# Turning the queries of two tiles with one DMA transpose in an attention and ReGLU kernel

## The chip, the core and the metric

The kernel runs on one core of a Trainium2 chip. The metric is the device time of one launch in microseconds (us). Before the change the median of three runs is 1029.53 us (1028.31 to 1029.58).

## The reference

Attention with keys and values that are pooled in space, followed by a feed-forward block with a ReLU gate. Everything has 128 channels:

```python
B, C, Hh, Ww = (4, 128, 384, 32)          # q: (4, 12288, 128), kv: (4, 384, 32, 128)
kv_pool = kv.reshape(B, H // r, r, W // r, r, C).mean(axis=(2, 4))   # r = 4
kv_flat = kv_pool.reshape(B, -1, C) @ w_sr                           # 768 rows for each image
k = v = kv_flat
s = scale * (q @ k.transpose(0, 2, 1))
a = np.exp(s - s.max(-1, keepdims=True))
a /= a.sum(-1, keepdims=True) + 1e-09
x = (a @ v).reshape(B * S, D)                                        # 49152 x 128
out = np.maximum(x @ w_gate, 0.0) * (x @ w_val) @ w_out              # d_ff = 1536
```

## The kernel before

The 49152 query rows are cut into 96 tiles of 512 rows (T), 24 for each image. Four tiles make a group (GRP), so there are 24 groups. `k` numbers tiles, `g = k // 4` groups, and `ph = k % 4` is the phase of a tile in its group.

**What happens to a tile.** Its queries are loaded from HBM by GpSimd's DMA, which casts them to float16 (`q_load`, L133, a whole group in four transfers, into the tile `q16`, two buffers). Rows lie on the partitions then, and the scores need the channels there, so the queries are turned by a DMA transpose on SyncE's queue (`q_turn`, L149, issued in L155) into `qT` (three buffers, a group each). Blocks of 128 queries are multiplied with the 768 keys (`score_block`, L359), ScalarE takes the exponential and its row sums (`exp_block`, L364), and the weights `a` are turned by two DMA transposes for each tile, on the same queue of SyncE (`a_turn`, L391), into `aT` (four buffers). TensorE multiplies them with the values (`values`, L401), VectorE stores the result as `xT` (L409), and then come twelve value and gate projections (L455, L468), their combination on ScalarE and VectorE (L462, L476), the product with w_out (L496), a transpose on VectorE (L504), the scaling on GpSimd (L509), and the store, by DMAs from SyncE and GpSimd (L741). The division by the row sums is put off to that scaling.

**What sets the order.** The order is written out by hand: lists of words say what each engine's queue gets next. The first four tiles are mixed into the opening, which also pools and projects the keys of the first image. Then a loop (L719) runs over steps `k` from 4 to 98, and each step deals with several tiles at different stages: the scores of tile `k`, the values of tile `k - 2`, the projections of tile `k - 3`, the output of tile `k - 4`. The lists are FIRST, STEADY and DRAIN. Beside this work, keys and values of the next image are loaded and pooled (`image_step`, L706) in the first half of each image's steps. Every queue runs its instructions in the order in which they are written here, and an instruction that waits holds up the ones behind it.

**The query turns.** They are issued at the head of a step, ahead of everything else that the step puts on SyncE's queue: the turned weights, half of the stores, the loads of keys and values. In the steps of group `g`, phase 1 turns tile 0 of group `g + 1`, phase 2 tile 1, phase 3 tile 2; tile 3 of a group is turned in phase 0 of its own steps. Groups 0 and 1 are partly turned in the opening, the rest of group 1 by one instruction at L722. In phase 1, after the turn, GpSimd's queue gets the loads of group `g + 2`, into the buffer of `q16` that the last turn of group `g` has read.

The lines which decide on that are these:

```python
        if ph == 0 and g > 1:
            q_turn(g, GRP - 1)
        elif ph > 0:
            q_turn(g + 1, ph - 1)
        if ph == 1:
            q_load(g + 2)
```

Of the kernel before, what the change touches and what calls it, by code (L numbers as in the profile page):

```python
# [16 lines left out]
def kernel(  # L17
# [34 lines left out]
    NS = T // 128  # L52
    NST = N // T
    NT = B * NST
    GRP = 4
# [77 lines left out]
    def q_load(g):  # L133
        if not 0 <= g < NG:
            return
        b, n0 = divmod(g * GRP * T, N)
        q16 = work.tile([128, GRP * NS, C], FP16, tag="q16", bufs=2)
        rows = q[b, n0 : n0 + GRP * T, :]
        if g == NG - 1:
            nc.gpsimd.dma_start(q16, rows.rearrange("(p s) c -> p s c", p=128))  # L140
        else:
            rows = rows.rearrange("(i t j s) c -> j t i s c", i=GRP, t=32, s=NS)
            for j in range(4):
                nc.gpsimd.dma_start(  # L144
                    q16[32 * j : 32 * (j + 1)].rearrange("t (i s) c -> t i s c", i=GRP), rows[j]
                )
        q16s[g] = q16

    def q_turn(g, i):  # L149
        if not 0 <= g < NG:  # L150
            return
        if g not in qTs:
            qTs[g] = work.tile([128, GRP * NS, 128], FP16, tag="qT", bufs=3, name="qT")
        at = slice(i * NS, (i + 1) * NS)
        nc.sync.dma_start_transpose(  # L155
            qTs[g][:, at], q16s[g][:, at].rearrange("p s c -> p (s c)")
        )
        if i == GRP - 1:
            del q16s[g]

    def q_load_pair(i):
# [218 lines left out]
    def spread_scales(k, j):  # L380
        if j == 0:
            scales[k // 2] = work.tile([128, 2, NS * 4], FP32, tag="scale", bufs=3, name="scale")
        to = scales[k // 2].rearrange("t e (s j) -> t e s j", j=4)
        for b in range(4):
            nc.gpsimd.tensor_copy(  # L385
                to[32 * b : 32 * (b + 1), :, :, j], squares[k // 2][32 * j : 32 * (j + 1)]
            )
# [99 lines left out]
    def out_proj(k, fb):  # L487
        if k >= NT - 3:
            if fb == 0:
                o_banks[k] = bank([128, NS, 128])  # L490
            for s in range(NS):
                out_add(k, fb, s, o_banks[k][:, s, :], fb == 0 and s == 0)
            return
        if fb == 0:
            o_banks[k] = bank([128, T])
        nc.tensor.matmul(  # L496
            o_banks[k], wo16[:, fb, :], hTs[k][:, fb, :], start=fb == 0, stop=fb == NFB - 1
        )

    def out_turn(k):  # L500


        o_t = work.tile([128, T], FP32, tag="o_t", bufs=2)
        nc.vector.transpose(o_t, freed(o_banks.pop(k)))  # L504
        o_sb = work.tile([128, 4, NS, 32], FP32, tag="o_sb", bufs=3)
        o_by = o_t.rearrange("t (s j c) -> t s j c", s=NS, j=4)
        to = o_sb.rearrange("t j s c -> t s j c")
        scale = scale_of(k).rearrange("t (s j o) -> t s j o", s=NS, o=1)
        nc.gpsimd.tensor_tensor(to, o_by, scale.to_broadcast([128, NS, 4, 32]), op=ALU.mult)  # L509
        del hTs[k]  # L510
        g = k // GRP
        rows = out[g * GRP * T : (g + 1) * GRP * T, :]
        moves = []
        for b in range(4):
            o_b = o_sb[32 * b : 32 * (b + 1)]
            if g == 0:
                to = rows.rearrange(
                    "(e j t i s) (b c) -> e b i j t s c", e=2, j=4, t=32, s=NS, c=32
                )
                moves += [(to[k // 2, b, k % 2, j], o_b[:, j]) for j in range(4)]  # L520
            elif g == NG - 1:
                to = rows.rearrange("(j t i s) (b c) -> b i j t s c", j=4, t=32, s=NS, c=32)
                moves += [(to[b, k % GRP, j], o_b[:, j]) for j in range(4)]
            else:
                to = rows.rearrange("(i t r) (b c) -> b i t r c", t=32, r=16, c=32)
                moves.append((to[b, k % GRP], o_b.rearrange("t j s c -> t (j s) c")))
        return moves

    def out_scale(k, engine, own, o_ps=None):
        if k not in o_sbs:  # L530
            o_sbs[k] = work.tile([128, NS, 128], FP32, tag="o_sb", bufs=3, name="o_sb")
        o_sb, o_ps = o_sbs[k][:, own], o_ps if o_ps is not None else freed(o_banks[k])
        scale = squares[k // 2][:, k % 2, own]
        if engine is nc.scalar:
            for s in range(o_sb.shape[1]):
                nc.scalar.mul(o_sb[:, s], o_ps[:, s], scale[:, s : s + 1])
        else:
            nc.vector.tensor_tensor(
                o_sb, o_ps, scale.rearrange("t (s o) -> t s o", o=1).to_broadcast(list(o_sb.shape)),
                op=ALU.mult,  # L540
            )
# [164 lines left out]
    def image_step(b, at, step):  # L706
        for pair in range(NJC // 2):
            since = at - 4 * pair
            if since in (0, 1) and step in (2, 8):
                kv_load(b, pair, [2 * since + step // 8])  # L710
            elif since in (3, 4) and step == 3:
                pool_pixels(nc.gpsimd, b, pair, since - 3)
            elif since == 6 and moves and step > 4:
                nc.sync.dma_start(*moves.pop())
            elif since in (9, 11) and step == 1:
                turn_values_dma(b, 2 * pair + since // 11)

    last = NT + LAG - 1
    for k in range(LEAD, last + 1):  # L719
        g, ph = divmod(k, GRP)  # L720
        if k == GRP:
            nc.sync.dma_start_transpose(  # L722
                qTs[1][:, 2 * NS :], q16s.pop(1)[:, 2 * NS :].rearrange("p s c -> p (s c)")
            )
        if ph == 0 and g > 1:
            q_turn(g, GRP - 1)
        elif ph > 0:
            q_turn(g + 1, ph - 1)
        if ph == 1:
            q_load(g + 2)  # L730
        b = k // NST + 1
        at = k % NST - 4
        kO, kF, kV = k - LAG - 1, k - LAG, k - 2
        words = FIRST if kV < LEAD else STEADY if k < NT else DRAIN if k < last else LAST
        for word in words:
            head, n = word.rstrip("0123456789"), int(word.lstrip("abcdefghijklmnopqrstuvwxyzADPT") or 0)
            if head == "o":
                out_proj(kO, n)
                for queue in (nc.gpsimd, nc.sync):
                    if out_moves and n >= 2:  # L740
                        queue.dma_start(*out_moves.pop())  # L741
                if spread:
                    spread_scales(*spread.pop(0))
                if b < B:
                    image_step(b, at, n)
            elif head == "oT":
                if kO < NT - 3:
                    out_moves = out_turn(kO)
                elif k < last:
                    out_scale(kO, nc.vector, slice(0, NS))  # L750
                    out_store(kO, slice(0, NS))
            elif head in ("v", "y", "g", "h"):
                if kF < NT:
                    {"v": value_proj, "y": keep_value, "g": gate_proj, "h": gated}[head](kF, n)
            elif head in ("s", "e"):
                if k < NT:
                    {"s": score_block, "e": exp_block}[head](k, n)
                    if head == "e" and n % 2:
                        a_turn(k, n - 1, n + 1)
            elif head == "r":  # L760
                if LEAD < k <= NT and k % 2 == 0:
                    invert(k - 2)
                    spread += [(k - 2, j) for j in range(4)]
            elif head in ("tb", "P", "pk"):
                pair, since = divmod(at - 6 if head == "tb" else at - 8, 4)
                if b < B and 0 <= pair < NJC // 2 and since == 0:
                    if head == "tb":
                        moves.extend(turn_blocks(b, pair))
                    elif head == "P":
                        project(b, pair)  # L770
                    else:
                        keep_projected(b, pair)
            elif LEAD <= kV < NT:
                if head == "x":
                    values(kV, n)
                else:
                    keep_values(kV)
# [33 lines left out]
```

The softmax here doesn't subtract the row's maximum and nothing guards it: scores larger than these inputs give would overflow.

## Time and profile before

| | before |
|---|---|
| median of 3 runs | 1029.53 us |
| span of the profiled run | 1027.5 us |
| PE, ACT, DVE, POOL busy | 99%, 90%, 84%, 51% |
| DMA bytes | 153.51 MB |
| query turns in the loop (L155) | 88 |
| issue of one on SyncE's queue: shortest, median, longest | 1.19, 1.75, 5.27 us |
| issue to landing of one: shortest, median, longest | 2.5, 4.1, 10.7 us |
| weight turns (L391) | 184, median issue 1.47 us, median 4.8 us to landing |

PE is TensorE, ACT ScalarE, DVE VectorE, POOL GpSimd, and SP SyncE; a q behind a name (SPq) means the engine's queue of instructions, which also issues DMAs. The busy time of PE counts matmuls which overlap, so the question is not how busy it is but where it waits. A DMA has two times: how long its instruction holds the queue, and how long it is until the data has landed. In a group of the profile, "out<-in" are the program's names for what an instruction writes and reads, and "A <- B" in the list of waits means that A stood idle until B was done.

### The profile page before, as it was taken

What the parts mean: (1) busy time and instruction counts of PE and PEld (TensorE: products, weight loads), DVE (VectorE), ACT (ScalarE), POOL (GpSimd) and SP (SyncE); (2) the same over time, 40 slices, a digit from 0 to 9 for tenths busy, and PEclk for the clock granted to TensorE, in tenths of its full rate; (3) what the DMA queues carried; (4) which work ended last, traced back from release to release, by engine and by line L of the source; (5) the groups of instructions that cost most, each with busy time, mean ns of one, the idle gap of its engine ahead of it and who ended that gap; (6) DMA issues with size and microseconds to landing.
All of it is one profiled execution on the core that took longest, in us unless ns stands there. A gap on an engine that the chain in (4) does not pass through costs nothing.

```text
span 1027.5 us, 17571 instructions
## 1 busy us (share of the span) xinstructions
PE 1020.5 (99%) x5048; PEld 489.5 (48%) x5048; DVE 862.5 (84%) x1432; ACT 920.1 (90%) x1931; POOL 525.1 (51%) x1308
## 2 busy tenths in 40 slices
PE   9999999999999999999999999999999999999998
PEld 5444444444444444444444444444444444444445
DVE  2888888888888888888888888888888888888887
ACT  5999998899999999999999999989999999999986
POOL 3588766434446585535434856654334443343342
PEclk9999999999999999999999999999999999999999
DMA  9999998999998998979879899898696897867641
GB/s 327 155 160 162 182 186 141 143 150 148 140 171 170 192 169 167 159 125 141 129 123 209 152 178 190 157 144 140 120 141 108 144 129 123 130 122 110 113 83 43
DMA packets 476721, 153.51 MB, mean 149 GB/s; under 512 B 452944, under 2 KB 466768, under 8 KB 476624
## 3 DMA queue, kind: packets, MB, share of 16 engines
q1 hardware_dynamic: 454592, 126.08, 68.6%
q0 software_dynamic: 21600, 25.19, 17.2%
q10 hardware_dynamic: 432, 1.11, 0.3%
q8 instruction: 40, 0.66, 0.3%
q14 instruction: 57, 0.47, 0.2%
HBM read 53.94 MB, written 26.35 MB: 78 GB/s over the span
## 4 chain that ended last, share of the span: by engine, by line
PE 97%; DMA 2%; ACT 1%; issue 0%; SPq 0%; DVE 0%; DVEq 0%
PE bank_ps L455 24%; PE bank_ps L468 24%; PE bank_ps L496 23%; PE bank_ps L401 12%; PE wide_ps L359 11%; DMA aT<-a 1%; DMA q<-in_q_dram 1%; PE bank_ps L482 1%; PE bank_ps L344 1%; PE bank_ps L418 0%; PE bank_ps L270 0%; PE wide_ps L302 0%; ACT a L364 0%; PE bank_ps L284 0%; ACT val L462 0%
## 5 line engine op out<-in xcount | busy, mean ns | idle before, releaser
L476 DVE SCALAR_TENSOR_TENSOR hT<-bank_ps,val 128x512 f16<-128x512 f32 x1152 | 728.2, 680 | 105.6 <-PE bank_ps L468 84.0
L462 ACT CAST val<-bank_ps 128x512 f16<-128x512 f32 x1149 | 628.3, 595 | 45.6 <-PE bank_ps L455 25.0
L455 PE MATMUL bank_ps<-xT,wv 128*128 128x512 f16 x1152 | 420.5, 379 | 0.1
L468 PE MATMUL bank_ps<-xT,wg 128*128 128x512 f16 x1152 | 375.9, 379 | 0.0
L496 PE MATMUL bank_ps<-hT,wo 128*128 128x512 f16 x1116 | 348.4, 379 | 0.0
L364 ACT ACTIVATE a<-wide_ps 128x768 f16<-128x768 f32 x368 | 302.0, 821 | 44.9 <-PE wide_ps L359 44.9
L359 PE MATMUL wide_ps<-kv,qT 128*128 128x512 f16 x736 | 179.7, 326 | 0.1
L401 PE MATMUL bank_ps<-aT,kv 128*128 128x512 f16 x552 | 178.8, 379 | 0.7 <-DMA aT<-a 0.6
L496 PEld LDWEIGHTS <-wo 128*128 128x128 f16 x1116 | 109.2, 98 | 131.9 <-issue 0.7
L468 PEld LDWEIGHTS <-wg 128*128 128x128 f16 x1152 | 112.7, 98 | 122.4 <-issue 0.5
L509 POOL TENSOR_TENSOR o_sb<-o_t,scale 128x512 f32<-128x512 f32 x89 | 93.2, 1047 | 137.9 <-issue 120.2
L455 PEld LDWEIGHTS <-wv 128*128 128x128 f16 x1152 | 112.7, 98 | 106.0 <-issue 1.7
L385 POOL COPY scale<-square 32x8 f32<-32x8 f32 x736 | 141.2, 192 | 28.6
L741 POOL DMA_DIRECT2D out_dram<-o_sb x216 | 134.8, 627 | 19.0 <-POOL o_sb L509 13.0
L378 POOL TENSOR_TENSOR square<-inverse 128x8 f32<-128x8 f32 x46 | 9.3, 202 | 249.0 <-DVE inverse L376 249.0
L359 PEld LDWEIGHTS <-qT 128*128 128x128 f16 x736 | 72.0, 98 | 87.1 <-issue 0.4
L409 DVE CAST xT<-bank_ps 128x512 f16<-128x512 f32 x92 | 63.6, 691 | 32.4 <-PE bank_ps L401 32.4
L401 PEld LDWEIGHTS <-kv 128*128 128x128 f16 x552 | 54.0, 98 | 66.5 <-issue 1.6
L364 ACT ACTIVATION_READ_ACCUMULATOR a<-wide_ps 128x1 f32 x368 | 75.9, 206 | 0.0
L504 DVE STREAM_TRANSPOSE o_t<-bank_ps 128x512 f32<-128x512 f32 x93 | 65.4, 704 | 0.0
L144 POOL DMA_DIRECT2D q<-in_q_dram x84 | 46.7, 573 | 15.6 <-DMA qT<-q 14.7
L237 POOL TENSOR_TENSOR s<-kv_in 128x512 f32<-128x512 f32 x36 | 45.2, 1285 | 1.5 <-DMA kv_in<-in_kv_dram 0.8
(78 smaller groups left out, 205.8 us busy)
## 6 DMA issues: line engine op xcount, KB each, us to landing
kv_in<-in_kv_dram SPq DMA_DIRECT2D x42, 512.0 KB, 4.7
out_dram<-o_sb SPq DMA_DIRECT2D x177, 64.0 KB, 2.6
out_dram<-o_sb POOLq DMA_DIRECT2D x176, 64.0 KB, 4.3
q<-in_q_dram POOLq DMA_DIRECT2D x84, 128.0 KB, 6.6
aT<-a SPq DMA_TRANSPOSE x184, 4.8
kv_line<-in_kv_dram SPq DMA_DIRECT2D x4, 512.0 KB, 9.9
qT<-q SPq DMA_TRANSPOSE x91, 4.1
placed<-blocks SPq DMA_DIRECT2D x9, 128.0 KB, 1.9
```

What stands on the lines that cost most here:

```text
L359: nc.tensor.matmul(s_ps[:, j0 * 128 : j1 * 128], qT, kv16[:, b, j0:j1, 0:C], start=True, stop=True)
L364: nc.scalar.activation(a16s[k][:, s, :], s_banks.pop(s)[:, 0:J], AF.Exp, scale=qk_scale, accum_out=a_sums[k // 2][:, k % 2, s : s + 1],)
L385: nc.gpsimd.tensor_copy(to[32 * b : 32 * (b + 1), :, :, j], squares[k // 2][32 * j : 32 * (j + 1)])
L401: nc.tensor.matmul(x_banks[k], kv16[:, k // NST, jc, C : 2 * C], aT[:, jc], start=first, stop=x_left[k] == 0,)
L455: nc.tensor.matmul(proj_banks["v", k, fb], wv16[:, fb * 128 : (fb + 1) * 128], xTs[k], start=True, stop=True,)
L462: (nc.vector.tensor_copy if k < LEAD - 1 and fb == 5 else nc.scalar.copy)(vals[k, fb], freed(proj_banks.pop(("v", k, fb))))
L468: nc.tensor.matmul(proj_banks["g", k, fb], wg16[:, fb * 128 : (fb + 1) * 128], xTs[k], start=True, stop=True,)
L476: nc.vector.scalar_tensor_tensor(hTs[k][:, fb, :], freed(proj_banks.pop(("g", k, fb))), 0.0, vals.pop((k, fb)), op0=ALU.max, op1=ALU.mult,)
L496: nc.tensor.matmul(o_banks[k], wo16[:, fb, :], hTs[k][:, fb, :], start=fb == 0, stop=fb == NFB - 1)
L504: nc.vector.transpose(o_t, freed(o_banks.pop(k)))
L509: nc.gpsimd.tensor_tensor(to, o_by, scale.to_broadcast([128, NS, 4, 32]), op=ALU.mult)
L741: queue.dma_start(*out_moves.pop())
```

## The change

A query turn takes two neighbouring tiles at a time. It is issued in phase 1 (tiles 0 and 1 of the next group) and in phase 3 (tiles 2 and 3), and none in phases 0 and 2. It is meant to halve the number of these instructions on SyncE's queue, and it frees the buffer of a group's loaded queries in the step before the group's own steps begin, not in the first of them.

```diff
-    def q_turn(g, i):
+    def q_turn_two(g, i):
         if not 0 <= g < NG:
             return
         if g not in qTs:
             qTs[g] = work.tile([128, GRP * NS, 128], FP16, tag="qT", bufs=3, name="qT")
-        at = slice(i * NS, (i + 1) * NS)
+        at = slice(i * NS, (i + 2) * NS)
         nc.sync.dma_start_transpose(
             qTs[g][:, at], q16s[g][:, at].rearrange("p s c -> p (s c)")
         )
-        if i == GRP - 1:
+        if i == GRP - 2:
             del q16s[g]
...
-        if ph == 0 and g > 1:
-            q_turn(g, GRP - 1)
-        elif ph > 0:
-            q_turn(g + 1, ph - 1)
+        if ph % 2:
+            q_turn_two(g + 1, ph - 1)
         if ph == 1:
             q_load(g + 2)
```

## The prediction

> **What bounds the kernel now.** I read the page's busy shares first, then the busy time by stretches, the list of waits, and last the SyncE queue's timeline where that list pointed. From the page:
>
> ```profile
> PE 1020.5 (99%) x5048; PEld 489.5 (48%) x5048; DVE 862.5 (84%) x1432; ACT 920.1 (90%) x1931; POOL 525.1 (51%) x1308
> ...
> q1 hardware_dynamic: 454592, 126.08, 68.6%
> ...
> PE 97%; DMA 2%; ACT 1%; issue 0%; SPq 0%; DVE 0%; DVEq 0%
> ```
>
> TensorE is busy 99% of the span, and the chain that ended last runs over it for 97%. A busy TensorE need not be one at its peak, so I looked for the time that it really loses. The busy time by stretches (columns: stretch, its length, then busy time and count of PE, PEld, DVE, ACT, POOL, clock, DMA share, GB/s):
>
> ```profile
> 38.00:62.00 24.00, 23.89 (x116) 11.20 (x115) 21.10 (x35) 23.22 (x51) 12.74 (x22) 1.00 1.08 185
> 62.00:230.00 168.00, 167.35 (x807) 79.27 (x806) 143.37 (x239) 152.21 (x321) 108.78 (x247) 1.00 0.95 159
> 230.00:640.00 410.00, 409.98 (x1978) 194.09 (x1977) 350.57 (x580) 374.35 (x788) 226.00 (x550) 1.00 0.94 160
> 640.00:1000.00 360.00, 360.00 (x1737) 170.13 (x1735) 308.52 (x510) 328.75 (x691) 155.06 (x436) 1.00 0.77 127
> ```
>
> Between 38 and 1000 us TensorE is idle for 0.11 + 0.65 + 0.02 + 0.00 = 0.78 us. Shorter waits could hide under the overlapping ends of matmuls, so I also looked at the starts in the timeline: 512-column matmuls start 0.216 us apart, the first value product (L401) of one tile follows that of the tile before by 10.37 us almost everywhere (10.80 where a key projection is added), and the exceptions add up to 0.27 us near 55.6, 0.17 at 156, 0.81 at 187.7 and 0.25 near 427. So between opening and end at most 1.5 us are lost, and 0.98 of it (156 and 187.7) on turned weights, aT. Everything else is the matmuls' own pace, which the change doesn't touch.
>
> The waits name the one place where a transpose held TensorE, and the one where a query turn held anybody:
>
> ```profile
> POOL q L144 <- DMA qT<-q: 14.7, 3, 7.2
> ...
> PE bank_ps L401 <- DMA aT<-a: 0.6, 1, 0.6
> ```
>
> The SyncE queue around that stall (start, length, count of merged instructions):
>
> ```profile
> 167.53 3.32 SPq L391 DMA_TRANSPOSE aT<-a  x2
> 170.90 1.59 SPq L155 DMA_TRANSPOSE qT<-q  x1
> 172.58 1.65 SPq L741 DMA_DIRECT2D out_dram<-o_sb  x2
> 174.32 3.88 SPq L391 DMA_TRANSPOSE aT<-a  x2
> 178.37 4.49 SPq L155 DMA_TRANSPOSE qT<-q  x1
> ```
>
> Its instructions follow each other without a hole. The weights of tile 16 were ready when ScalarE ended its last exponential at 168.5, but their second turn was issued at 175.90 and landed 12.63 us later, at 188.5; the product that reads it started 0.65 us late. So from about 80 to 220 us the queue runs some 5 to 16 us behind its inputs. Taking landing times from the trace, the spare time between the landing of a tile's aT and its first reader is 0.1 us for tiles 13 and 16, 0.9 to 1.3 for 8, 10, 12 and 14, 2.6 and 2.7 for 15 and 9; the median over all tiles is 11.7, and from tile 22 on it is never under 7.
>
> **What the Trainium skill says.** "DMA: Bandwidth & Descriptors", section "Rules for kernel authors", advises to coalesce many small transfers into a large one. A one-tile turn moves 128x512 float16, 131 KB, a joint one 262 KB, so only the fixed part is to be saved. "Perfetto Trace Analysis", section "DMA Instruction — HWDGE (DVE, Sync)", says that such an instruction's profiled time is the generation of its descriptors and not the moving, and that its wait is done by the sequencer before it. The trace agrees: the shortest query turn takes 1.19 us on the queue and 2.5 us to landing. "DMA: Bandwidth & Descriptors", section "Issuing engines are not separate DMA queues", says that GpSimd's and SyncE's transfers share the same engines; here the aT turn at 175.90 landed after 12.63 us, against a median of 4.8, just when GpSimd's four query loads had been issued from 175.64.
>
> **The change part by part.**
>
> *Fewer instructions.* Groups 2 to 23 have 4 turns each, the row's 88; now 2 each, 44. Bytes stay. Lone issue time hardly depends on size: at best 1192 ns for the 4 blocks of a query turn, 1273 ns for the 12 of an aT turn, so 10 ns for a block and 1.23 us for 8 blocks. That is the lower bound of a joint turn. The upper one: the queue is held back by the engines. q1 moved 126.08 MB in 68.6% of 1027.5 us, 179 GB/s, so 131 KB more cost 0.73 us; added to the median single turn of 1.745 us this gives 2.48 us. Two single ones take 3.49, so a pair saves 1.0 to 2.2 us of queue time, 44 pairs 44 to 99 us; I take 1.5, 66 us. Off the path nearly everywhere: TensorE waits for this queue once. It counts only in the backlog from 62 to 230 us, some 16 steps and 8 pairs: 8 to 18 us saved there, as much as the backlog itself. So I expect the spare times there to grow by some us, and the 0.65 us stall (0.81 by the starts) to shrink or vanish.
>
> *Where the turns stand.* Before: tile 0 of the next group at phase 1, 1 at phase 2, 2 at phase 3, 3 at phase 0 of its own group. Now 0 and 1 at phase 1, 2 and 3 at phase 3. No tile is turned later than before; each is turned three or four steps (31 or 41 us) ahead of its scores, against a longest landing of 10.7 us. No reader gets a new wait: 0. The buffers: qT's third one was last read a group earlier (0), and the query load that a joint turn needs was issued four steps before (landing at most 10.8 us): 0.
>
> *What waits behind.* In phases 1 and 3 the joint turn stands ahead of that step's two aT turns; these come up to 0.73 us later by it. In phases 0 and 2 they come 1.2 to 1.75 us earlier. On balance a gain: of the six tiles with under 1.3 us to spare, five are in phases 0 and 2 and only tile 13 in phase 1, with a whole turn (1.56 us at 126.57) gone from the step before it.
>
> *The query load.* q_load(g+2) at phase 1 takes the buffer that the last turn of group g frees. That turn now stands two steps earlier, so GpSimd's three waits, 3.33, 7.25 and 4.09 us, 14.7 together, end. GpSimd is 51% busy and nobody is named as waiting for it on the path, so this is worth 0 directly. But these three loads go out earlier, and each is a burst that stretches aT turns. This part I cannot size from the trace of before; both ends follow below.
>
> *Sum.* −0.65 us times a good chance that it goes, about −0.5, and nothing else on the path: 1029.53 − 0.5 = 1029.0 us.
>
> **The rivals.**
>
> *A: the load's burst hits a tight tile.* The load of group 6 moves from 175.64 to 168.4, into the landing of tile 15's turns (issued 167.53 and 169.10, read at 177.50). If the second takes 12.63 us as tile 16's did, it lands at 181.7: 4.2 us of stall instead of 0.65, so 1029.53 + 3.6 = 1033.1 us, slower than before by 0.3%. For it: the collision is the very one that caused the stall before. Against it: the queue by then issues these turns 1 to 3 us sooner, before the load, and the other two moved loads (3.33 and 4.09 us earlier) newly meet tiles (11 and 19) with over 6 us to spare. A milder form, 1 to 2 us on one or two tiles, gives 1030 to 1031.5.
>
> *B: all waits in the steady part vanish.* Then 1.5 us go, 1028.0 us, still within 0.2%. Only the 0.98 us on aT has anything to do with the change, so this needs luck in the waits at 55.6 and 427 too.
>
> *C: faster by over 0.2%.* This needs 2.06 us, more than TensorE loses between 38 and 1000 us. Opening and end have no part that the change moves: the first changed turn is issued at about 49 us, and the last turn only moves from 952 us to some 10 us before. Only scatter of the runs (1028.31 to 1029.58) could show it.
>
> *D: single waits shift but the sum stays.* 1029.5 us; it cannot be told from my forecast.
>
> **How the numbers follow.** Forecast with D: 0.72, at 1029.0. B: 0.10. A in its mild form: 0.07; A in full, or a stall like it elsewhere, over 1031.6: 0.08. C: 0.03. The range from 1027.8 (B less a little of the scatter) to 1031.2 (most of mild A) leaves out C, full A and a little at the edges, some 0.14. The bounds on the joint turn's issue (1.23 to 2.48 us) don't widen it, as both save queue time. Faster by over 0.2% 0.04, within 0.2% 0.86, slower 0.10.
>
> **What would show it.** Right: 44 turns of 8 blocks with a median issue between 1.23 and 2.48 us; no wait of GpSimd's query load for a query turn; the three loads issued near 126, 168 and 211 us; TensorE still busy 99%, tiles still 10.37 us apart; no or less wait for aT; DMA bytes as before. Wrong: waits of L401 for aT of several us between 60 and 230 us (A), a joint turn holding the queue over 3.5 us in the median, so that nothing is saved, or scores (L359) waiting for qT.

## The result, and the profile after

The change makes the kernel faster: 1026.62 us in the median of 12 runs (1026.31 to 1027.44), against 1029.55 us (1028.20 to 1031.37) for the kernel before, a ratio of 0.9975 with a 95% interval of 0.9967 to 0.9983. That is 2.9 us less. The forecast was 1029.0 us with a range of 1027.8 to 1031.2, and "faster by over 0.2%" had a chance of 0.04. Beside the median, the spread shrank, from 3.2 to 1.1 us.

From the page of the kernel after:

```profile
PE 1019.4 (100%) x5048; PEld 489.5 (48%) x5048; DVE 861.8 (84%) x1432; ACT 919.9 (90%) x1931; POOL 524.8 (51%) x1308
...
q1 hardware_dynamic: 453184, 126.08, 67.7%
...
PE 98%; DMA 1%; ACT 1%; SPq 0%; issue 0%
```

The bytes of q1 are the same, and so is the work of every engine. The busy time by stretches of the kernel after (same columns as in the prediction):

```profile
38.00:62.00 24.00, 23.89 (x117) 11.24 (x115) 21.09 (x36) 23.16 (x51) 12.22 (x22) 1.00 1.02 195
62.00:230.00 168.00, 168.00 (x812) 79.82 (x810) 144.13 (x241) 153.00 (x322) 109.07 (x248) 1.00 0.94 164
230.00:640.00 410.00, 409.98 (x1978) 194.05 (x1977) 350.50 (x579) 374.40 (x788) 225.29 (x549) 1.00 0.91 159
640.00:1000.00 360.00, 360.00 (x1736) 170.12 (x1735) 308.30 (x510) 328.23 (x690) 155.94 (x439) 1.00 0.74 125
```

In the second row TensorE's 167.35 us have become 168.00 of 168.00. In the list of waits, GpSimd's query load no longer waits for a turn, and the value product no longer waits for aT. In a second profile of this kernel (below) it does not either. The query turns themselves, all instructions of line 155 (shortest, median and longest time on the queue, in ns, then issue to landing):

```profile
L155 SPq DMA_TRANSPOSE qT<-q x44: 1314/1784/5349, 48.2 to 939.8; - x44
...
DMA to landing us min/median/max: 3.4/5.5/9.1
```

A joint turn holds the queue for 1.78 us in the median, where a single one took 1.75. Summed over the trace, query turns take 88.6 us of SyncE's queue instead of 174.9. Part of that is taken up again: between 62 and 230 us, all instructions that issue DMAs together held the queue for 152.8 us of the 168 before, and for 141.0 and 143.9 us in the two profiles after, as the weight turns then took longer. The queue at the place that the prediction showed:

```profile
162.18 3.32 SPq L391 DMA_TRANSPOSE aT<-a  x2
165.59 1.52 SPq L739 DMA_DIRECT2D out_dram<-o_sb  x2
167.20 4.59 SPq L391 DMA_TRANSPOSE aT<-a  x2
171.97 5.35 SPq L155 DMA_TRANSPOSE qT<-q  x1
```

Tile 16's two weight turns now start at 167.20 and 168.89; they started at 174.32 and 175.90. The second one landed 8.5 us before its reader, where it had held the reader up.

**Where the 3.0 us between the two profiled spans went.** The first value products of the tiles in the loop, L401, are good marks, as TensorE's order is the same in both kernels.

| stretch | before | after | difference |
|---|---|---|---|
| start to the first L401 | 62.46 us | 61.68 us | -0.78 |
| first L401 to that of the last tile | 940.67 us | 939.70 us | -0.97 |
| that one to the end | 24.38 us | 23.16 us | -1.22 |

The middle row is what the prediction hoped to gain from, and its size is what was allowed there. Two thirds, 2.00 us, lie in the start and the end. Both profiled executions took about their kernel's median (1029.29 and 1026.33 us of launch time), so the table can stand for a typical execution. There were two questions for the experiments: is 0.97 us the usual loss of the kernel before, and do the start and the end have anything to do with the change?

### The profile page after: what moved, and what is told of

Its sections match the earlier page's. It is cut to its first block, busy times and chain, and to the rows that moved or that the text cites. A ratio compares the mean times of both kernels' runs of the same rounds, so it can differ in the third digit from the quotient of the medians.

```text
span 1024.5 us, 17514 instructions
## 1 busy us (share of the span) xinstructions
PE 1019.4 (100%) x5048; PEld 489.5 (48%) x5048; DVE 861.8 (84%) x1432; ACT 919.9 (90%) x1931; POOL 524.8 (51%) x1308
## 3 DMA queue, kind: packets, MB, share of 16 engines
q0 software_dynamic: 21600, 25.19, 15.9%
## 4 chain that ended last, share of the span: by engine, by line
PE 98%; DMA 1%; ACT 1%; SPq 0%; issue 0%
PE bank_ps L455 24%; PE bank_ps L468 24%; PE bank_ps L496 23%; PE bank_ps L401 12%; PE wide_ps L359 12%; DMA q<-in_q_dram 1%; PE bank_ps L482 1%; PE bank_ps L344 1%; PE bank_ps L418 1%; PE bank_ps L270 0%; PE wide_ps L302 0%; PE bank_ps L284 0%; ACT a L364 0%; ACT val L462 0%; PE bank_ps L432 0%
## 5 line engine op out<-in xcount | busy, mean ns | idle before, releaser
L401 PE MATMUL bank_ps<-aT,kv 128*128 128x512 f16 x552 | 178.9, 379 | 0.0
L401 PEld LDWEIGHTS <-kv 128*128 128x128 f16 x552 | 54.0, 98 | 65.1
```

What stands on the lines that cost most here:

```text
L401: nc.tensor.matmul(x_banks[k], kv16[:, k // NST, jc, C : 2 * C], aT[:, jc], start=first, stop=x_left[k] == 0,)
```

## The experiments

### The kernel before once more

No edit.

> The kernel before, unchanged, for a second profile. The gain of 2.9 us splits in the two profiles into 0.78 us before the first value product of the loop (L401), 0.97 us between the first and the last tile's, and 1.25 us after it. If the first and the last part are properties of the program, this profile has them as before: first L401 near 62.5 us, some 24.4 us from the last tile's first L401 to the end, and a ratio of 1.000. If they are scatter of single executions, they move here by some tenths of a us or more, and only the 0.97 us need an explanation from the program.

Measured: 1029.07 us, ratio 0.9999 (0.9992 to 1.0005). The start takes 62.46 us and the end 24.23 us, much as before. But the middle took 942.09 us, 2.4 us more than 939.70. The waits of TensorE in this profile (total, times, longest) and the busy time from 62 to 230 us:

```profile
PE bank_ps L401 <- DMA aT<-a: 1.9, 3, 1.2
```

```profile
62.00:230.00 168.00, 166.09 (x800) 78.49 (x799) 142.25 (x237) 151.03 (x318) 110.17 (x249) 1.00 0.93 159
```

The same program, and TensorE idles three times instead of once, before tiles 8, 12 and 13; in the first profile it idled before tile 16, and tile 13 came 0.17 us late. What follows: the loss is drawn anew in each execution. It does not follow that the first profile had an unusually small one. The second profiled execution took 1030.57 us, 1.5 us more than the median of its own kernel, and the first 1029.29 us. If the 1.5 us lie in the middle, where the two profiles differ, a typical execution loses some 0.9 us there (2.39 less 1.5, an estimate).

### Joint turns early, joint turns late

```diff
-        if ph == 0 and g > 1:
+        if ph == 0 and g > 1 and not (g < 6):            # late: not (g >= 6)
             q_turn(g, GRP - 1)
-        elif ph > 0:
+        elif ph > 0 and not (g + 1 < 6):                 # late: not (g + 1 >= 6)
             q_turn(g + 1, ph - 1)
+        elif ph % 2:
+            q_turn(g + 1, ph - 1, 2)                     # two tiles
```

(`q_turn` takes the number of tiles as its third argument here.)

> Joint turns for groups 2 to 5 alone (8 instructions fewer), single ones from group 6 on. Theory 1 (queue time of SyncE in the backlog up to 230 us): the aT stalls go, 0.98 us less between first and last L401, 1028.6 us. Theory 2 (the end of the program: semaphores of the last DMAs and instruction fetches, which shift with the count of DMAs; 8 fewer leave the eight semaphores in the same turn): the end stays at 24.4 us here, and the gain is no more than 1 us. If the whole gain of 2.9 us came from the early stretch, it would be 1026.6 us.

> Joint turns from group 6 on alone (36 instructions fewer, which moves the last DMAs by four of the eight semaphores as the change does). Theory 1: the stall before tile 16 and the slip before tile 13 stay, no gain between first and last L401. Theory 2: the end gets 0.3 to 1.2 us shorter, 1028.4 to 1029.3 us. If both hold, this gain and that of the early pairs add up to about 2.2 of the 2.9 us.

Measured: early pairs 1027.64 us, ratio 0.9983 (0.9974 to 0.9992); late pairs 1028.78 us, ratio 0.9993 (0.9984 to 1.0001). From 62 to 230 us, first of the early pairs, then of the late ones:

```profile
62.00:230.00 168.00, 168.00 (x812) 79.90 (x811) 144.07 (x240) 153.00 (x322) 109.23 (x249) 1.00 0.91 165
```

```profile
62.00:230.00 168.00, 165.11 (x795) 78.03 (x794) 141.26 (x234) 150.17 (x316) 108.17 (x246) 1.00 0.94 156
```

Eight instructions fewer in groups 2 to 5 remove every stall in this profile: the middle takes 939.70 us, to the hundredth what it takes in the kernel after. (One of the 18 executions took 1034.72 us; nothing was recorded of what held it up.) The gain, 1.6 us in the medians, is not that of the middle alone. The profiled execution took 1027.69 us, 1.60 us less than the one before; of this the middle has 0.97 us, the start 0.46 and the end 0.72 us. Against them stands launch time outside the profiled span: in all 18 executions it was 2.2 to 2.3 us, and 1.7 to 2.0 us in all executions of every other kernel. Where this half microsecond goes, no run shows. With late pairs the middle keeps its stalls (943.07 us), and the start and the end, 61.83 and 23.23 us, are about those of the kernel after. So the stalls belong to the early groups; the start and the end are shorter in both. 1.6 and 0.5 us add up to 2.1 of the 2.9 us, but such gains need not add up.

### The same places, but one tile each

```diff
-        if ph == 0 and g > 1:
-            q_turn(g, GRP - 1)
-        elif ph > 0:
-            q_turn(g + 1, ph - 1)
+        if ph % 2:
+            q_turn(g + 1, ph - 1)
+            q_turn(g + 1, ph)
```

> The turns where the change has them (phases 1 and 3), but one instruction for each tile, 88 as before. Theory 1 (fewer instructions on the queue): the backlog stays and so do stalls of tiles 13 and 16, perhaps larger as two turns stand in a row in phases 1 and 3: 1029.5 us or slower. Rival (the earlier release of the loaded queries' buffer, so that GpSimd's waits of 14.7 us for a turn end): the stalls go here as with the change, 0.98 us less between first and last L401, 1028.6 us. Count of DMAs as before, so the end stays at 24.4 us.

Measured: 1030.32 us, ratio 1.0013 (1.0001 to 1.0025), slower than before if anything. TensorE waits for aT before tiles 13 and 15; the middle takes 941.78 us.

```profile
PE bank_ps L401 <- DMA aT<-a: 1.8, 2, 1.2
```

It is not the places that help, nor the earlier release of the buffer that comes with them, but that there are fewer instructions. (The 16 single turns between 62 and 230 us held the queue for 23.3 us here, less than the 36.1 before, but the weight turns for 73.6 instead of 65.5, and the queue as a whole was hardly freer.)

### A third buffer for the loaded queries

```diff
-        q16 = work.tile([128, GRP * NS, C], FP16, tag="q16", bufs=2)
+        q16 = work.tile([128, GRP * NS, C], FP16, tag="q16", bufs=3)
```

(and the same in the other place that names the tile.)

> The kernel before, with three buffers for the loaded queries in place of two: GpSimd's wait for a turn (14.7 us in three times) goes, the loads of groups 5 to 7 go out 3 to 7 us earlier as with the change, and nothing else differs, one turn for each tile. Theory 1 (queue time): no gain, 1029.2 us, stalls in tiles 8 to 16 as before. Rival (the release): 1 to 2 us less. Third case (the moved loads hurt tile 15 as feared in the prediction): a stall at tile 15, 1030 us or more.

Measured: 1028.31 us, ratio 0.9997 (0.9986 to 1.0008): no gain can be told, and the interval reaches from 1.4 us of gain to 0.8 of loss. The loads of groups 5 to 7 go out at 125.9, 167.8 and 212.4 us, near the kernel after's 125.5, 167.4 and 209.3 us. TensorE's timeline of this profile where it stalls:

```profile
179.66 0.38 PE L401 MATMUL bank_ps<-aT,kv 128*128 128x512 f16 x1 [2.51 <-DMA aT<-a]
```

This is tile 15, whose weight turns were in flight when the load of group 6 came 7.8 us earlier than before: the rival A of the prediction, with 2.5 us of its 4.2. This execution was a slow one, 1030.28 us, 2.0 us over the median of its kernel. In the kernel after, the same load at the same time did no harm in either profile: tile 15's turns had landed 8.7 and 4.0 us ahead of their reader.

### Giving the queue time back

The kernel after, with tiny stores to a scratch tensor that nobody reads.

```diff
+        if 4 < k <= 20 and ph % 2 == 0:                  # second run: if 4 < k <= 20
+            for n in range(2):                           # second run: range(3)
+                tiny = dram.tile([1, 128], FP32, tag="tiny", bufs=8, name="tiny")
+                nc.sync.dma_start(tiny, ident[0:1, :])
         if ph == 1:
             q_load(g + 2)
```

> The kernel after, with two tiny stores of 512 bytes each (one row of the identity, to a scratch tensor that nobody reads) put on SyncE's queue at the head of the steps 6, 8, ... 20, where the change took a turn away: 16 instructions, almost no bytes. It gives back queue time (about 0.6 us each, 9 us together) without load on the DMA engines. If the gain is the queue time saved in the backlog, spare times of tiles 8 to 16 fall back to under 2 us and stalls return: 1 to 2.5 us between first and last L401, 1027.6 to 1029 us. If the gain comes from elsewhere (fewer transposes in flight, the earlier release of the query buffer), the time stays at 1026.6 us and the spare times stay above 4 us. 16 more instructions leave the eight semaphores in the same turn, so the end stays at about 23.2 us.

Measured: 1026.68 us in the median, ratio to the kernel before 0.9984 (0.9974 to 0.9993), no stall in the profile, 939.70 us in the middle. I had expected stalls. The 16 stores held the queue for only 6.9 us in all, not the 9 us expected. But 3 of the 22 executions took 1032.2 to 1032.9 us, where none of the 22 executions of the kernel after was over 1027.44; these three were not profiled. How far the queue is behind can be read for each tile from its second aT turn: start of the turn less the end of the exponential that it waits for. The longest such lag was 9.2 and 11.0 us in the two profiles of the kernel after, and is 10.4 us here, so it shows no effect of the stores; in the kernel before it was 14.0. Hence a larger dose.

> As the fill before, but three stores of 512 bytes in every step from 5 to 20: 48 instructions, 24 KB in all, some 27 us of queue time. The first fill raised the longest lag of a tile's second aT turn behind its exponentials from 9.2 to 10.4 us, while the profiles with stalls have 13.6 to 16. If the lag is what decides, 48 stores take it past 13 us, stalls come back at tiles 8 to 16, 1 to 5 us between first and last L401, and the time is 1027.6 to 1032 us with the wide scatter of the kernel before. If stalls come from the turns on the DMA engines and not from the queue, the time stays at 1026.7 us. End as in the kernel after, 23.2 us (48 is six times the eight semaphores).

Measured: 1032.55 us (1029.83 to 1036.45), ratio to the kernel before 1.0030 (1.0018 to 1.0042). In the profile, which is that of the slowest of the 16 executions, the longest lag is 15.9 us, and the middle takes 948.97 us.

```profile
PE bank_ps L401 <- DMA aT<-a: 6.9, 4, 3.1
```

```profile
62.00:230.00 168.00, 161.08 (x768) 75.56 (x766) 137.10 (x228) 144.78 (x305) 107.22 (x244) 0.99 0.89 153
```

The 48 stores hold the queue for 19.2 us, about what the change had taken from it. Their 24 KB are little beside the 26 MB that the DMA engines move between 62 and 230 us, and yet they make the kernel after slower than the kernel before, with more stalls than that one and a wider scatter.

### Queue time from another source

The kernel before, its turns untouched:

```diff
-                for queue in (nc.gpsimd, nc.sync):
+                for queue in (nc.gpsimd, nc.gpsimd if 8 < k <= 20 else nc.sync):
                     if out_moves and n >= 2:
                         queue.dma_start(*out_moves.pop())
```

> The kernel before, query turns untouched, but in the steps 9 to 20 all output stores are issued by GpSimd's queue in place of every second one by SyncE: 24 instructions, about 15 us of SyncE's queue time, the same bytes on the same DMA engines. Theory 1 (the queue's time in the backlog decides, whoever gives it back): longest lag under 10 us, no stalls, 939.70 us between first and last L401, 1027.6 us as with the early pairs. Rival (only fewer or larger transposes help): stalls stay, 1029.2 us. 24 fewer leave the semaphores in the same turn, so the end stays above 23.6 us.

Measured: 1026.90 us, ratio 0.9985 (0.9977 to 0.9993), 2.2 us less by the medians, without touching a query turn. The expectations of no stall at all and of a lag under 10 us (13.1 us at tile 10) were wrong for this profile:

```profile
106.05 0.38 PE L401 MATMUL bank_ps<-aT,kv 128*128 128x512 f16 x1 [2.31 <-DMA aT<-a]
```

That is tile 8. Its second turn is issued in step 8, before the relief begins; it was issued at 92.2 us, among the loads of group 4 (from 91.4 us), and landed 13.7 us later. The profiled execution, with 1029.87 us, was 3.0 us over the median, so a stall like this is not the rule. For tiles 12 to 20 the lag is 0.1 to 9.9 us, against 5.2 to 14.0 in the kernel before, and nothing stalls. Moving stores off the queue and joining turns on it have the same effect on these tiles, and small stores put on it the opposite one; it is the queue's time. A long lag alone is not a stall: tile 10, with 13.1 us, had 1.4 us to spare here.

### The end of the program

```diff
+        if k == 80:
+            pad = dram.tile([4, 128, 128], FP32, tag="pad", bufs=1, name="pad")
+            for n in range(4):
+                nc.sync.dma_start(pad[n], ident)
         b = k // NST + 1
```

> The kernel before, with four more stores of 64 KB from the identity to a scratch tensor on SyncE's queue in step 80, where it has over 10 us to spare. Four more DMAs turn the eight semaphores to where the change has them. If that turn shortens the end, the time from the landing of the last store to the end of the program falls from 1.94 us by 0.26 us (four waits of 0.065 us that come after the last landing, not before it), and by more if the holes of 0.3 us in it go as well; the rest of the kernel stays as before, with its stalls: 1028.5 to 1029.0 us. If the shorter end has to do with the turns themselves, it stays at 1.94 us and 1029.2 us.

> The kernel after, unchanged, for a second profile. If its even times come from a queue that never lets TensorE wait, first to last L401 is 939.70 us again, without a slip; end 23.2 us; the start up to the first L401 may lie anywhere between 61.5 and 62.5 us, as it has in the profiles so far. Time 1026.6 us.

> The kernel after, with four stores of 64 KB from the identity to a scratch tensor on SyncE's queue in step 80, which turn the eight semaphores back to where the kernel before has them. In the kernel before four stores the other way shortened the time from the last landing to the end from 1.94 to 1.36 us, one hole of 0.3 us remaining. If the turn is the cause, that time rises here from 1.05 to 1.3 us (four waits of 0.065 us), or to 1.6 or 1.9 us if one or two holes come as well; between first and last L401 nothing changes, 939.70 us. Time 1026.9 to 1027.5 us. If the end is short for another reason, it stays at 1.05 and the time at 1026.6 us.

Measured: four stores in the kernel before give 1028.74 us, ratio 0.9991 (0.9983 to 1.0000); the kernel after again 1026.65 us, ratio 0.9975 (0.9965 to 0.9984); four stores in the kernel after 1026.61 us, ratio 0.9977 (0.9967 to 0.9987).

DMAs issued by SyncE and ScalarE signal on eight semaphores in turn, as the trace of the issues shows. At its end SyncE waits for all of them, in a fixed order, each some 0.065 us after the one before. With 44 DMAs fewer the last ones move by four places, 44 being 4 over a multiple of 8: the last store's semaphore was second in the order and is now sixth, so that four more of the waits are over before it lands. Times from the trace:

| profile | last landing to the end | holes in it |
|---|---|---|
| before, twice | 1.94 us | one of 0.34 us on SyncE's queue, one of 0.35 us on GpSimd's |
| before with four stores | 1.36 us | one on GpSimd's |
| one tile each in the new places | 1.60 us | one on GpSimd's |
| early pairs | 1.42 us | none of this kind; SyncE ends its drain 0.3 us later than elsewhere |
| late pairs | 1.04 us | none |
| after, twice | 1.05 and 1.04 us | none |
| after with four stores | 1.29 us | none |
| stores moved to GpSimd | 1.29 us | none |
| one turn for a whole group (below) | 0.92 us | none |

Where there is neither a hole nor a late drain, the place of the last semaphore alone tells the time: 1.29 us when it is second, 1.04 or 1.05 when sixth, 0.92 when eighth (the last row). Turned back by four stores, the end of the kernel after is longer by 0.25 us, the 0.26 us expected, with nothing changed in the middle (939.70 us). The medians, 1026.65 and 1026.61 us, cannot tell so little apart. The holes, an engine's queue that does nothing for 0.3 us and waits for nothing that the profile shows, come and go from program to program. The kernels before and after differ by one packet of the instruction queue (57 and 56), but the one with stores moved to GpSimd has 57 and no hole, so what they are was not settled.

What shortens the start is not shown. It is 62.46 us in both profiles of the kernel before and 61.48 to 62.13 us in all twelve others, so it need not be scatter; but one of the twelve is the kernel before with four stores at step 80 (61.68 us), an edit that cannot act on it through its instructions. Nor can the changed turns: of the 0.78 us, 0.77 are there at 37 us, when the first product with w_out starts (37.43 us before, 36.66 after), and the first changed turn is issued at 48.2 us.

### One turn for a whole group

```diff
+        if ph == 1:
+            q_turn(g + 1, 0, GRP)
             q_load(g + 2)
```

(in place of the other turns.)

> One turn for a whole group, in phase 1 of the group before: 22 instructions in place of 44. If queue time counts, another 1 us for each group is saved, but the spare times of the kernel after are already above 4 us, so nothing more is to be had: 1026.3 to 1027.0 us. If one long transpose in front of the turned weights of phase 1 hurts, tiles 9, 13 and 17 lose their spare time and stalls come back, 1027 to 1030 us. 22 fewer turn the semaphores by two places.

Measured: 1026.60 us, ratio 0.9973 (0.9964 to 0.9982): no different from the change. The middle is at 939.70 us, but tile 13 has only 0.2 us to spare, and the longest lag is back at 13.1 us; a long turn ahead of phase 1's weights costs what the saved instructions bring. There is nothing left in the middle of the profile for such a version to gain.

### All profiles side by side

"Held" is the time between 62 and 230 us in which instructions that issue DMAs held SyncE's queue, summed over the trace; "lost" is the time between the first and the last L401 over 939.70 us; "rest" is the launch time of the profiled execution outside these two marks.

| profile | held | lost | rest |
|---|---|---|---|
| late pairs | 154.7 us | 3.37 us | 86.88 us |
| before with four stores | 153.0 us | 3.49 us | 87.08 us |
| before, twice | 152.8 us, both | 0.97 and 2.39 us | 88.62 and 88.48 us |
| third buffer | 152.2 us | 2.67 us | 87.91 us |
| after with 48 stores | 151.0 us | 9.27 us | 87.48 us |
| one tile each in the new places | 150.4 us | 2.08 us | 87.80 us |
| one turn for a whole group | 147.3 us | 0 | 87.01 us |
| stores moved to GpSimd | 144.6 us | 2.47 us, at tile 8 | 87.70 us |
| after, twice | 141.0 and 143.9 us | 0 | 86.63 and 87.08 us |
| after with 16 stores | 143.8 us | 0 | 86.44 us |
| after with four stores | 142.5 us | 0 | 86.84 us |
| early pairs | 137.2 us | 0 | 87.99 us |

A queue that is held for 150 us or more of the 168 goes with stalls, one of 147.3 us or less with none, but for tile 8 ahead of the relief. The sum does not tell how large a stall is. The last column is a caution: the kernel before has the longest rest of all, and every edit, whatever it did, shortened it by 0.5 to 2.2 us. Times against the kernel before contain that; the middle shows the queue alone.

## Why the prediction was wrong

**The bound** was right. TensorE sets the pace; 939.70 us from the first to the last tile is what it takes without a wait for aT, and six profiles, of the kernel after, its variants and the early pairs, come to that figure.

**The mechanism** was right for the middle. The prediction named the backlog of SyncE's queue from 62 to 230 us, the stalls of the value product behind it, and the queue time that joint turns give back. All of the queue's numbers fell within their bounds: a median issue of 1.78 us (1.23 to 2.48 forecast), and 86 us saved in all (44 to 99, 66 taken). In the stretch from 62 to 230 us it was 36.1 us less 18.6, so 17.5 us (8 to 18), of which the whole queue kept 8.9 to 11.8 us.

**The step that failed** is the term for the two ends of the program. "Opening and end have no part that the change moves" put it at nothing, and on it rests the dismissal of rival C, "This needs 2.06 us, more than TensorE loses between 38 and 1000 us". In the two profiles the ends have 2.00 of the 2.97 us. They do so in the second profiles too: the rest of the execution outside the middle is 88.62 and 88.48 us before, 86.63 and 87.08 us after. The reason given, that no changed instruction stands there, was true and not enough. The end fell by 1.22 us: 0.25 us by the turn of the semaphores, which hangs on how many DMAs the whole program has; about 0.65 us by holes that went; and the rest by the last store landing 1.73 us after ScalarE's last instruction, not 2.05 or 1.90. For the holes and the landing there is no shown cause. The start fell by 0.78 us, ahead of any changed instruction, and its cause stays open.

**A second term was mis-sized**, the gain in the middle. The forecast took about 0.5 us from it; what went was 0.97 us in the profiles, all that turned weights had cost there, and within the "at most 1.5 us" that the prediction allowed. That figure held for a typical execution, not for each one. Four profiles whose early part is that of the kernel before (before twice, late pairs, and four stores at step 80) lose 0.97, 2.39, 3.37 and 3.49 us. The last three come from executions that were 1.50, 1.17 and 1.53 us over the median of their own kernel; taken off, they leave 0.9, 2.2 and 2.0 us, an estimate that puts all of this excess into the middle. Six tiles stood within 1.3 us of their readers, and different ones are late in different profiles, each adding a loss of its own. The prediction had a sign of it in hand: it listed those spare times, but took the scatter of the runs (1.3 us in the three known then) for that of the measurement. With the stalls gone, the spread over 12 runs fell from 3.2 to 1.1 us.

**Rival A** did not come about, for the reason that was given against it. But the profile with three buffers suggests that the reason was needed: with the load moved and the queue still late, tile 15 stalled for 2.5 us.

**What stays open.** That queue time ends the stalls is shown; how the 2.9 us divide is known only roughly, some 1 us from the middle and some 2 us from the ends by the profiles that lie near the medians. The late pairs do not fit into a plain sum: their start and end are about those of the kernel after, and yet their median gained only 0.5 us (1.6 us to none by the interval), so that their middle seems to lose more than that of the kernel before. An earlier start may leave the queue less time before its first tight reader; no run tests this.

## What to carry to other kernels

Where an in-order DMA queue runs late and several readers stand within a microsecond of their data, one trace shows one draw of the stalls; take a second profile, set each against the median of its kernel, and ask how many tight places there are. In this kernel queue time counted from whatever source it came, fewer and larger transposes or stores issued elsewhere. A wait that is removed elsewhere can be a loss while the queue is still late. And a forecast of a few tenths of a per cent has to allow for the start and the end, which here moved by 2 us though no changed instruction stands in them.

## What the runs showed of the hardware

A DMA transpose of 8 blocks of 128x128 held the queue for about as long as one of 4, 1.78 and 1.75 us in the median, and either could take up to 5.3 us. 48 stores of 512 bytes in 16 steps held the queue for 19.2 us and cost 5.9 us over the kernel that they were added to (1032.55 less 1026.65, medians of different sets of runs). And four DMAs more, at step 80 of the kernel after, made its end 0.25 us longer, through the semaphore on which the last one signals.
